# Score matmuls of 64 rows by 128 columns issued as 64 by 32 tiles

## Chip, cores and metric

The kernel runs on one core of a Trainium2 chip. The metric is the device time of one execution in microseconds (us), the median of several runs. A profile is taken of one further execution; its instruction trace is what the views below are read from.

## What is computed

One sequence of 2048 tokens with 512 channels goes through two attention blocks with 32 heads of 16 channels each. Block A is a linear attention with softmax features, block B is ordinary softmax attention. A gate per token mixes them. Cut to what matters:

```python
x = A_x                                              # [1, 2048, 512], bf16
g = sigmoid((x * gate_w).sum(-1, keepdims=True))
a = A(x)      # linear attention: phi(q) (phi(k)^T v) / (phi(q) . sum phi(k)), then @ A_wo
# B(x):
q, k, v = split_heads(x @ B_wqkv)                    # 32 heads, 16 channels
scores = einsum("bhqd,bhkd->bhqk", q, k) * 16 ** -0.5
p = softmax(scores, axis=-1)
b = einsum("bhqk,bhkd->bhqd", p, v) @ B_wo
out = g * a + (1 - g) * b
```

The 32 x 2048 x 2048 exponentials of block B are most of the work.

## The kernel before

**Work of block B.** The queries are cut into four chunks of 512. The heads stand in four groups of eight (`g`), and each group is gone through in two halves (`par`), so there are 32 "sets" of four heads and 512 queries (`N_SETS`). In each set the 16 tiles of 128 keys (`kt`) are gone through in two halves (`cc`), which makes 32 x 16 x 2 = 1024 score groups.

A score group (`qk`, L1103 to L1109, matmul on L1106) makes the scores of two heads: for each head 128 keys by 512 queries, into one PSUM bank per head. Keys of eight heads lie on the 128 partitions of `kT`. The queries lie in `qz`, spread out so that a slot holds one head of each half of the partitions and zeros elsewhere. One matmul uses the 64 partitions 0 to 63 (head half h = 0), the other 64 to 127 (h = 1). `tile_position=(64 * h, 0)` places each on its own half of the rows of the TensorE array, with all 128 columns of the array as output rows.

The exponential of the scores is made in one of two ways. For most key tiles ScalarE makes it (L1116), one instruction for the two banks of a group, from PSUM to the bf16 buffer `E`. For up to six of the 16 key tiles of a set VectorE makes it by arithmetic on the bit pattern: two instructions (L1121) per group, one for each bank, into the int16 buffer `T`, and two shifted copies `TS` (L1129), so that three terms stand for one exponential.

The value matmuls (`pv`, L1143) follow: four matmuls side by side, each with all 128 rows and a strip of 32 columns of the array (`tile_position=(0, 32 * col)`), which accumulate into the bank `psO`. A column of ones beside the values gives the sum for the softmax. A group of these is due once for each key tile that ScalarE made and three times for each one that VectorE made. At a set's end `psO` is copied out (L770), transposed by a DMA and normalised (L1169, L1170).

**PSUM.** Seven banks (`psR`) are shared by score groups, projections and all else; the eighth is `psO`. A score group for ScalarE takes two neighbouring banks, one for VectorE any two.

**The rest.** Projections of q, k, v (L787 and L849), the features of block A (L979 on ScalarE, L985 to L995 on POOL), its output (L1055), the output projection (L1205), a sum for a check of the value range (L927), and the gate (L892, one output column per matmul) are set in between as full 128 x 128 matmuls.

**What sets the order.** A planner in the program (`_Sched`) places every operation on an engine before the program is built, from a list of costs and due times written in the code: a score group counts 0.22 us, an exponential of ScalarE 0.905, a change of tiling on TensorE 0.11 (`SWITCH`). It writes one fixed list per engine; each engine runs its list in that order and waits on semaphores for what an operation needs. An operation made of several matmuls waits ahead of the first and signals with the last. The costs in the planner are not changed, so neither are the lists.

Of the kernel before, what the change touches and what calls it, by code (L numbers as in the profile page):

```python
# [101 lines left out]
class _Sched:  # L102
# [5 lines left out]
    def add(self, eng, prio, occ, fn, deps=(), tiles=(), mode=None, name="", lat=None, dma=None, lane=None, nb=0.0,  # L108
            kind=None, run=None, alt=None):
        o = _Op()  # L110
        o.alt = alt
        o.eng, o.fn, o.occ, o.prio = eng, fn, occ, prio
        o.lat = {"pe": 0.17, "act": 0.12, "dve": 0.09, "pool": 0.1, "sp": 0.0}[eng] if lat is None else lat
        if dma is not None:
            o.lat = dma
        o.deps = [d for d in deps if d is not None]
        o.tiles = list(tiles)
        o.mode, o.name, o.dma, o.lane, o.est, o.kind, o.run = mode, name, dma, lane, nb, kind, run
        o.users, o.start, o.end, o.count, o.sem, o.vc = [], None, None, None, None, None
        o.seq = len(self.ops)  # L120
        for t in o.tiles:
            t.ops.append(o)
        self.ops.append(o)
        return o
# [502 lines left out]
def _build(ctx, nc, A_x, A_wqkv, A_w_phi, A_wo, B_wqkv, B_wo, gate_w, out):  # L627
    cnt = [0]

    def sb(shape, dt=BF16, name="sb"):  # L630
        cnt[0] += 1
        return ctx.enter_context(nc.sbuf_tensor(f"{name}_{cnt[0]}", shape, dt))
# [13 lines left out]
    kT = sb([128, KT, S], name="kT")  # L646
# [52 lines left out]
    def pair(ts):  # L699
        return banks[:, ts[0].idx:ts[0].idx + 2, :]  # L700

    def st_(x):
        return T0 + P_SET * x
# [297 lines left out]
    for qd in range(4):  # L1001
# [13 lines left out]
        for lo in (0, 4):  # L1015
# [4 lines left out]
                start=(i == 0), stop=(i == 3)) for g in range(lo, lo + 4) for i, it in enumerate(items)]  # L1020
# [58 lines left out]
    for s in range(N_SETS):  # L1079
        qc, g, par = s // 8, (s // 2) % 4, s % 2  # L1080
# [5 lines left out]
        qt = q_t[g, qc]  # L1086
# [5 lines left out]
        for eng, frac, kt in todo:  # L1092
            alt = ((s, kt), eng) if kt in dset else None
            pr = st_(s + frac)
            T, T1, T2 = (_Tile(T_r), _Tile(TS_r), _Tile(TS_r)) if eng == "dve" else (None, None, None)
            exps, es = [], []
            for cc in range(2):
                rs = [_Tile(B_r), _Tile(B_r)]
                if eng == "act":
                    rs[0].mate, rs[1].mate = rs[1], rs[0]  # L1100
                c = 2 * par + cc

                def qk(e, rs=rs, c=c, kt=kt, g=g, qt=qt):  # L1103
                    ins = None
                    for h in range(2):
                        ins = e.matmul(rs[h].ap, lhsT=kT[64 * h:64 * h + 64, g, 128 * kt:128 * (kt + 1)],  # L1106
                                       rhs=qt.ap[64 * h:64 * h + 64, c, :], start=True, stop=True, tile_position=(64 * h, 0))
                    return ins
                q = add("pe", pr + 0.5 * cc, 0.22, qk, deps=[ev_k[g, kt // 4]] + (op_qz[g, qc] if len(op_qz[g, qc]) == 8 else [op_qz[g, qc][c]]), tiles=rs + [qt], mode="row",  # L1109
                        name=f"qk{s}.{kt}", kind="qk", run=eng, alt=alt)  # L1110
                if s == N_SETS - 1 and eng == "act":
                    tail_qk.append(q)
                if eng == "act":
                    E = _Tile(E_r)
                    es.append(E)
                    exps.append(add("act", pr + 0.5 * cc, 0.905, lambda e, rs=rs, E=E: e.activation(  # L1116
                        E.ap.rearrange("p (a n) -> p a n", n=512), pair(rs), ACTF.Exp, scale=SCALE),
                                    deps=[q], tiles=rs + [E], name="exp", kind="exp", alt=alt))
                else:
                    for h in range(2):  # L1120
                        exps.append(add("dve", pr + 0.5 * cc + 0.01 * h, 0.6, lambda e, rs=rs, T=T, cc=cc, h=h: e.tensor_scalar(  # L1121
                            T.ap[:, 1024 * cc + 512 * h:1024 * cc + 512 * h + 512], rs[h].ap,
                            ACC, BIAS, op0=ALU.mult, op1=ALU.add),
                            deps=[q], tiles=[rs[h], T], name="expd", kind="exp" if h else "exp0", alt=alt))
            if eng == "act":
                rounds = [(exps, lambda cc, es=es: es[cc].ap, lambda hd, kt=kt: vB[:, kt, hd, :], [], es)]
            else:
                di = DSET.index(kt)
                s1, s2 = (add("dve", pr + 1.0 + 0.3 * m, 0.6, lambda e, T=T, X=X, m=m: e.tensor_single_scalar(  # L1129
                    X.ap, T.ap, SHIFT[m], ALU.add), deps=exps, tiles=[T, X], name="sh", kind="sh", alt=alt) for m, X in ((1, T1), (2, T2)))  # L1130
                rounds = [(exps, lambda cc, T=T: T.ap[:, 1024 * cc:1024 * (cc + 1)].bitcast(BF16), lambda hd, kt=kt: vB[:, kt, hd, :], [], [T]),
                          ([s1], lambda cc, T=T1: T.ap[:, 1024 * cc:1024 * (cc + 1)].bitcast(BF16),
                           lambda hd, di=di: vS[:, 0, di, hd, :], [op_vS[g, kt // 4, 0]], [T1]),
                          ([s2], lambda cc, T=T2: T.ap[:, 1024 * cc:1024 * (cc + 1)].bitcast(BF16),
                           lambda hd, di=di: vS[:, 1, di, hd, :], [op_vS[g, kt // 4, 1]], [T2])]
            for ri, (dps, rhs, lhs, more, holds) in enumerate(rounds):
                def pv(e, rhs=rhs, lhs=lhs, g=g, par=par, O=O, s=s, key=(kt, ri)):
                    ins = None
                    for cc in range(2):
                        for h in range(2):  # L1140
                            col = 2 * h + cc
                            hd = 8 * g + 4 * h + 2 * par + cc
                            ins = e.matmul(O.ap[32 * col:32 * col + VW, :], lhsT=lhs(hd), rhs=rhs(cc)[:, 512 * h:512 * (h + 1)],  # L1143
                                           start=(first_pv[s] == key), stop=(last_pv[s] == key), tile_position=(0, 32 * col),
                                           skip_group_check=True)
                    return ins
                o = add("pe", pr + 2.5 - 40.0 * (s == N_SETS - 1), 0.22, pv, deps=list(dps) + [ev_v[g, kt // 4], op_psO] + more, tiles=holds + [O], mode="col",
                        name=f"pv{s}.{kt}.{ri}", kind="pv", alt=alt)
                o.run = (s, (kt, ri))
                pvs.append(o)  # L1150
# [153 lines left out]
```

## Time and profile before

| | |
|---|---|
| median of 3 runs | 748.07 us (747.75 to 748.65) |
| the profiled execution | 749.46 us, span of its instructions 747.6 us |
| mean granted TensorE clock | 0.992 of full speed |
| L1106 score matmuls | 2048, mean 386 ns, together 347.5 us of TensorE time |
| L1106 weight loads for them | 2048, mean 93 ns |
| L1143 value matmuls | 1452 + 1192 + 596, mean 382 to 384 ns |
| L1116 exponentials on ScalarE | 726, mean 1120 ns |
| L1121 first terms on VectorE | 596, mean 683 ns |

How to read it: PE is TensorE, PEld its weight loads, DVE is VectorE, ACT is ScalarE, POOL is GpSimd. Tile names read out<-in: `psR<-qz,kT` are the score matmuls, `psO<-E,vB` value matmuls. Matmuls are pipelined and the end of each is modelled, so the 386 ns of one matmul are its passage through the array, and several overlap; what one adds is read from the distance of the starts. The chain is the work that ended last, followed back from the last instruction: each step goes to what released it or to the instruction before it on its engine.

### The profile page before, as it was taken

To read this page: it belongs to the slowest core of one execution; us is meant where nothing else is said; L and a number is where in the kernel's file an instruction comes from. 1 tells how busy PE (TensorE), PEld (TensorE's weight loads), DVE (VectorE), ACT (ScalarE), POOL (GpSimd) and SP (SyncE) were. 2 spreads that over 40 slices of the span, in tenths; PEclk is the share of its full clock that TensorE was granted. 3 is DMA by queue.
4 is the path that set the end of the run, shared out by engine and by line. 5 is a ranking of instruction groups with operands and counts; after the bars stand their busy time and mean duration, and the time that the engine had idled before them with its cause. 6 is when DMAs were issued, how large, how long until landed. Compare 5 with 4: busy or idle time off the path is not lost.

```text
span 747.6 us, 15606 instructions
## 1 busy us (share of the span) xinstructions
PE 695.1 (93%) x6432; PEld 216.0 (29%) x6432; DVE 693.4 (93%) x1212; ACT 711.6 (95%) x803; POOL 193.7 (26%) x234
## 2 busy tenths in 40 slices
PE   7999999999999989988989999998989999988886
PEld 3333342332322222222222332222222322222222
DVE  3989899999999999999999999999999999999993
ACT  3999799999999999999999999999999999999993
POOL 4165241233344343322322012222212112200000
PEclk8999999999999999999999999999999999999999
DMA  8300000011000000001211221211111211111001
GB/s 210 73 16 9 8 16 15 15 41 33 15 15 15 8 14 10 15 16 30 48 31 30 50 50 36 44 33 33 22 36 40 47 36 37 32 27 8 16 8 32
DMA packets 72157, 23.77 MB, mean 32 GB/s; under 512 B 64016, under 2 KB 72080, under 8 KB 72080
## 3 DMA queue, kind: packets, MB, share of 16 engines
q1 hardware_dynamic: 70736, 22.19, 13.9%
q8 instruction: 52, 0.85, 0.5%
q10 hardware_dynamic: 1344, 0.52, 0.3%
q14 instruction: 25, 0.20, 0.1%
HBM read 4.21 MB, written 2.10 MB: 8 GB/s over the span
## 4 chain that ended last, share of the span: by engine, by line
ACT 65%; PE 26%; DVE 5%; DMA 2%; SPq 1%; issue 0%; DVEq 0%
ACT E L1116 62%; PE psR L1106 10%; PE psO L1143 6%; PE psR L787 4%; PE psR L1205 3%; DVE T L1121 2%; PE psR L849 2%; ACT WAT L979 2%; ACT phk L979 1%; DMA OTT<-OT 1%; DVE TS L1129 1%; SPq L706 1%; DMA T<-in_A_x_dram 1%; PE psR L927 1%; DVE ob L1170 1%
## 5 line engine op out<-in xcount | busy, mean ns | idle before, releaser
L1116 ACT ACTIVATE E<-psR 128x1024 bf16<-128x1024 f32 x726 | 679.8, 1120 | 17.2 <-PE psR L1106 15.8
L1121 DVE TENSOR_SCALAR T<-psR 128x512 int16<-128x512 f32 x596 | 380.8, 683 | 20.8 <-PE psR L1106 16.3
L1106 PE MATMUL psR<-qz,kT 64*128 64x512 bf16 x2048 | 347.5, 386 | 38.3 <-ACT E L1116 28.0
L1129 DVE TENSOR_SCALAR TS<-T 128x2048 int16<-128x2048 int16 x298 | 193.2, 684 | 3.1
L1106 PEld LDWEIGHTS psR<-qz,kT 64*128 64x128 bf16 x2048 | 87.0, 93 | 306.6 <-ACT E L1116 221.3
L1143 PE MATMUL psO<-E,vB 128*18 128x512 bf16 x1452 | 127.1, 382 | 0.0
L1143 PE MATMUL psO<-TS,vS 128*18 128x512 bf16 x1192 | 105.6, 382 | 0.6 <-DVE TS L1129 0.6
L1143 PE MATMUL psO<-T,vB 128*18 128x512 bf16 x596 | 58.7, 384 | 0.0
L985 POOL TENSOR_TENSOR WAT<-WAT 128x512 f32<-128x512 bf16 x16 | 18.5, 1156 | 148.0 <-DVE TS L1129 105.6
L990 POOL TENSOR_TENSOR tr<-WAT 128x256 f32<-128x256 f32 x32 | 23.4, 733 | 94.5 <-DVE TS L1129 94.5
L1143 PEld LDWEIGHTS psO<-E,vB 128*18 128x18 bf16 x1452 | 31.3, 88 | 51.3 <-issue 37.1
L995 POOL TENSOR_TENSOR phk<-phk,ss 128x1024 bf16<-128x1024 bf16 x16 | 30.9, 1930 | 51.5 <-DVE TS L1129 51.5
L995 POOL TENSOR_TENSOR WAT<-WAT,ss 128x1024 bf16<-128x1024 bf16 x16 | 30.9, 1930 | 48.5 <-DVE TS L1129 48.5
L1143 PEld LDWEIGHTS psO<-TS,vS 128*18 128x18 bf16 x1192 | 26.6, 87 | 53.3 <-issue 29.5
L787 PE MATMUL psR<-Wp,xT 128*128 128x512 bf16 x128 | 33.2, 382 | 0.8 <-DVE T L1121 0.8
L787 PE MATMUL psR<-xT,WB 128*128 128x512 bf16 x128 | 33.2, 382 | 0.4 <-ACT WAT L979 0.2
L985 POOL TENSOR_TENSOR WAT<-phk 128x512 f32<-128x512 bf16 x16 | 18.7, 1166 | 31.2 <-DVE TS L1129 31.2
L1143 PEld LDWEIGHTS psO<-T,vB 128*18 128x18 bf16 x596 | 14.5, 87 | 27.9 <-issue 21.4
L862 POOL TENSOR_SCALAR vS<-vB 128x144 bf16<-128x144 bf16 (+1 forms) x32 | 11.9, 373 | 39.4 <-DVE TS L1129 34.0
L770 DVE CAST OT<-psO 128x512 bf16<-128x512 f32 x31 | 21.1, 681 | 0.1
L979 ACT ACTIVATE phk<-psR 128x512 bf16<-128x512 f32 x32 | 18.6, 675 | 0.8 <-PE psR L787 0.8
L979 ACT ACTIVATE WAT<-psR 128x512 bf16<-128x512 f32 x32 | 19.1, 709 | 0.0
(108 smaller groups left out, 379.7 us busy)
## 6 DMA issues: line engine op xcount, KB each, us to landing
qz<-qst SPq DMA_DIRECT2D x120, 16.0 KB, 1.8
out_dram<-WAv SPq DMA_DIRECT2D x12, 128.0 KB, 1.7
WB<-in_B_wqkv_dram SPq DMA_DIRECT2D x3, 384.0 KB, 6.7
T<-in_A_x_dram SPq DMA_DIRECT2D x2, 512.0 KB, 5.3
WAv<-in_A_wqkv_dram SPq DMA_DIRECT2D x1, 512.0 KB, 8.3
WB<-in_A_wo_dram SPq DMA_DIRECT2D x1, 512.0 KB, 3.9
WB<-in_B_wo_dram SPq DMA_DIRECT2D x1, 512.0 KB, 3.6
OTT<-OT SPq DMA_TRANSPOSE x31, 2.4
```

The lines of the kernel that those rows point to most:

```text
L770: return add("dve", prio, 0.6, lambda e: e.tensor_copy(dst(), src()), deps=deps, tiles=tiles, name=name)
L787: calls = [lambda e, t=t: e.matmul(tile.ap[:, off:off + 512], lhsT=lhs(t), rhs=rhs(t), start=(t == 0), stop=(t == KT - 1)) for t in range(KT)]
L979: ex = [add("act", prio, 0.48, lambda e, s=s: e.activation(ev()[:, :, 16 * s:16 * s + 16], P(), ACTF.Exp, scale=1.0 - 2.0 * s), deps=[f] + ...
L985: p1 = pool(prio + 2, 1.23, lambda e: e.tensor_tensor(v8(), eg()[:, :, 0:8], eg()[:, :, 8:16], ALU.add), ex + use_wat, tiles=[ee, tr], nam ...
L990: p2 = pool(prio + 2, 0.92, lambda e: e.tensor_tensor(u4(), v8()[:, :, 0:4], v8()[:, :, 4:8], ALU.add), [p1], tiles=[tr, tr2])
L995: return pool(prio + 6, 1.95, lambda e: e.tensor_tensor(eg(), eg(), ss.ap[:, 1, :].unsqueeze(2).to_broadcast([128, 64, DH]), ALU.mult), [o ...
L1106: ins = e.matmul(rs[h].ap, lhsT=kT[64 * h:64 * h + 64, g, 128 * kt:128 * (kt + 1)], rhs=qt.ap[64 * h:64 * h + 64, c, :], start=True, stop= ...
L1116: exps.append(add("act", pr + 0.5 * cc, 0.905, lambda e, rs=rs, E=E: e.activation(E.ap.rearrange("p (a n) -> p a n", n=512), pair(rs), ACT ...
L1121: exps.append(add("dve", pr + 0.5 * cc + 0.01 * h, 0.6, lambda e, rs=rs, T=T, cc=cc, h=h: e.tensor_scalar(T.ap[:, 1024 * cc + 512 * h:1024 ...
L1129: s1, s2 = (add("dve", pr + 1.0 + 0.3 * m, 0.6, lambda e, T=T, X=X, m=m: e.tensor_single_scalar(X.ap, T.ap, SHIFT[m], ALU.add), deps=exps, ...
L1143: ins = e.matmul(O.ap[32 * col:32 * col + VW, :], lhsT=lhs(hd), rhs=rhs(cc)[:, 512 * h:512 * (h + 1)], start=(first_pv[s] == key), stop=(l ...
L1205: calls = [lambda e, tile=tile, off=off, sl=sl, src=src, w=w, n=n: e.matmul(tile.ap[:, off:off + 512], lhsT=src.ap[:, n % 4, sl], rhs=w[:, ...
```

## The change

Each of the two matmuls of a score group is cut into four along the 128 keys, which are the columns of the array. Each of the four has its own weight load of 32 columns and runs on a tile of 64 rows by 32 columns at `(64 * h, 32 * j)`. It streams the same 64 partitions by 512 queries and writes 32 partitions of the same PSUM bank as before. The two heads alternate.

```diff
                 def qk(e, rs=rs, c=c, kt=kt, g=g, qt=qt):
                     ins = None
-                    for h in range(2):
-                        ins = e.matmul(rs[h].ap, lhsT=kT[64 * h:64 * h + 64, g, 128 * kt:128 * (kt + 1)],
-                                       rhs=qt.ap[64 * h:64 * h + 64, c, :], start=True, stop=True, tile_position=(64 * h, 0))
+                    for j in range(4):
+                        for h in range(2):
+                            ins = e.matmul(rs[h].ap[32 * j:32 * j + 32, :], lhsT=kT[64 * h:64 * h + 64, g, 128 * kt + 32 * j:128 * kt + 32 * j + 32],
+                                           rhs=qt.ap[64 * h:64 * h + 64, c, :], start=True, stop=True, tile_position=(64 * h, 32 * j))
                     return ins
```

## The prediction

> **What bounds the kernel now.** I read the page's engine sums and its chain first, then the groups, the waits, and last the TensorE timeline around 302 us.
>
> ```profile
> span 747.6 us, 15606 instructions
> PE 695.1 (93%) x6432; PEld 216.0 (29%) x6432; DVE 693.4 (93%) x1212; ACT 711.6 (95%) x803; POOL 193.7 (26%) x234
> ...
> ACT 65%; PE 26%; DVE 5%; DMA 2%; SPq 1%; issue 0%; DVEq 0%
> ACT E L1116 62%; PE psR L1106 10%; PE psO L1143 6%; PE psR L787 4%; PE psR L1205 3%; DVE T L1121 2%; PE psR L849 2%; ACT WAT L979 2%; ACT phk L979 1%; DMA OTT<-OT 1%; DVE TS L1129 1%; SPq L706 1%; DMA T<-in_A_x_dram 1%; PE psR L927 1%; DVE ob L1170 1%
> ...
> L1116 ACT ACTIVATE E<-psR 128x1024 bf16<-128x1024 f32 x726 | 679.8, 1120 | 17.2 <-PE psR L1106 15.8
> L1106 PE MATMUL psR<-qz,kT 64*128 64x512 bf16 x2048 | 347.5, 386 | 38.3 <-ACT E L1116 28.0
> ```
>
> ScalarE is busy for 711.6 of 747.6 us and holds 65% of the chain that ended last: the exponentials of L1116 bound the kernel. TensorE holds 26% of that chain, so in about a quarter of the span its own order of work is late and ScalarE waits for it or is about to. The score matmuls (L1106), the only ones that change, are 10% of the chain, about 75 us.
>
> From the list of waits:
>
> ```profile
> PEld psR L1106 <- ACT E L1116: 221.3, 520, 0.8
> ...
> PEld psR L1106 <- DVE T L1121: 30.0, 94, 1.8
> ```
>
> Each row is total us, times, longest. There are 2048/2 = 1024 score groups of two matmuls. Some 520 + 94 = 614 of them begin when ScalarE or VectorE gives a PSUM bank back, not when TensorE gets to them. Up to such a wait, lateness gathered on TensorE is forgiven.
>
> The timeline of TensorE shows what a group costs (start, length of the merged piece, count):
>
> ```profile
> 302.31 0.39 PE L1106 MATMUL psR<-qz,kT 64*128 64x512 bf16 x2
> 302.63 0.39 PE L1143 MATMUL psO<-TS,vS 128*18 128x512 bf16 x4
> 302.85 0.39 PE L1143 MATMUL psO<-E,vB 128*18 128x512 bf16 x4
> 303.17 0.61 PE L1106 MATMUL psR<-qz,kT 64*128 64x512 bf16 x4
> 304.14 0.39 PE L1106 MATMUL psR<-qz,kT 64*128 64x512 bf16 x2 [0.37 <-ACT E L1116]
> 304.47 1.04 PE L787 MATMUL psR<-Wp,xT 128*128 128x512 bf16 x4
> 305.44 0.39 PE L1106 MATMUL psR<-qz,kT 64*128 64x512 bf16 x2
> ```
>
> Two things are to be seen. A second score group adds 0.61 - 0.39 = 0.22 us, and a second value group (L1143) starts 302.85 - 302.63 = 0.22 after the first, though one holds two matmuls and the other four: the tiles of a group run side by side. A step between tilings takes longer: 302.63 - 302.31 and 303.17 - 302.85 are 0.32, 304.47 - 304.14 is 0.33. So a change of tiling costs about 0.10 us, and it costs that also from 64x128 to 128x128 tiles (304.14 to 304.47), where the rows of a tile alone change.
>
> **The change part by part.**
>
> *Count.* Each of the 1024 score groups goes from 2 matmuls and 2 weight loads to 8 and 8: 6144 more of each, 12,576 of each on TensorE in all. The written order of all five engines is unchanged (one list per engine; only the members of a score group multiply), and so are the waits: the first matmul of a group waits, the last one signals. No DMA of the program, no tile and no buffer changes. VectorE, ScalarE and POOL do the same instructions.
>
> *Streaming.* If all eight 64x32 tiles run side by side the group still streams 512 columns, the 0.22 of above. The trace has no 64x32 tile. It has two row tiles beside each other (L1106) and four column tiles beside each other (L1143: four matmuls in one 0.39 piece). I cost the stream at nothing. If it does not hold, that is the second rival below.
>
> *Start of the later tiles.* Counting TensorE's instructions in 10 ns windows around the value group that starts at 301.71 gives x2, x4, x6 (two of each belong to the score group before), so its four matmuls start inside 20 ns: some 3 to 4 ns apart. In a score group the second starts within 10 ns. Eight tiles at 3 to 4 ns put the last one 21 to 28 ns behind the first, where it is 4 ns now: **+20 ns** on the group's end. From below this is 0, if starts got closer; from above the nearest row is L892, 32 pairs of load and one-column matmul in 0.95 us, less the 0.16 that one of them takes to pass: 0.79/31 = 25 ns a pair, which would make 7 x 25 - 4 = +171 ns. I take 20, since L1143 is the column-tiled stream and L892 reuses one tile, so each must follow the one before.
> The Trainium skill (TensorE: Matmul & The Clock Gate, Measured speedup vs the span model) gives about 4 ns per added tile; by it the six added tiles cost 24 ns, and the sum below would be 6.0 us in place of 5.0.
>
> *Weight loads.* Steps into a value group (four loads of 18 columns) and into a score group (two of 128) both take 0.32, so neither count nor width of loads shows. Eight of 32 columns I cost at 0, bounded by the 10 ns that two such steps differ by.
>
> *Switches.* A score group is still tiled otherwise than the value matmuls (64 against 128 rows) and than the projections. Rows alone differing cost 0.33 above, so no switch goes: 0.
>
> *Instruction supply.* The two instruction queues carried 1.05 MB for 15,606 instructions in the whole span, at 0.6% of the DMA engines. 12,288 more add about 0.8 MB. TensorE must then be handed 25,152 in 747.6 us, one every 30 ns, where it is 58 now. Cover: the densest piece seen, L892, takes one every 12.5 ns. If that pace is not sustained, the first rival follows.
>
> *What reaches the end.* 75 us of score matmuls on the chain at 0.22 (no switch) to 0.32 (switch) a group are 235 to 340 groups; most stand at a switch, so about 250. Each ends 20 ns later: 250 x 0.020 = **5.0 us**, and this is a floor if 20 ns holds, since the order is fixed and the chain is only lengthened. The ceiling is all groups, 1024 x 0.020 = 20.5. Groups off the chain are mostly those 614 that start at a released bank; there the 20 ns is hidden by ScalarE's next exponential (L1116, 1120 ns), whose input lies ready. Some groups between them will join the chain, as from 37 to 75 us, where 25 of 52 groups wait for a bank (from 300 to 338 us it is 47 of 55). I add 1.5 us for these, near the floor because more than half of the groups wait. Sum +6.5: the profiled execution took 749.46 around its span of 747.6, and goes to 756.0; against the median 748.07 of the runs shown this is 754.5.
>
> **The rivals.**
>
> 1. *TensorE is not handed instructions fast enough.* For: 16 per group in place of 4, and rows show no stretch longer than 64 instructions at the dense pace. Against: steps of 3 ns in value groups, and no wait on TensorE in the page that nothing explains. Price at L892's 25 ns a pair: +171 ns on 250 groups, 43 us, so 791; on all 1024, 175 us, so 923. The same page of the Trainium skill (Wait — 56ns, not 53.3ns?) states about 62 ns per matmul where instructions are decoded by the sequencer's code. An estimate by that page is 8 x 62 = 496 ns a group, and the time would pass 900; no run here shows which decoding is in use.
>
> 2. *The two row halves do not run together once columns are split.* Then a group takes two passes, +0.21 us: 250 x 0.21 = 53, so 801; on all, 218, so 966. For: no row has both kinds at once. Against: each kind alone runs at full overlap.
>
> 3. *Nothing reaches the end.* The 20 ns ends in the 614 waits each time, or starts get closer together: below 1.5 us, 748. Against: the chain has about 250 such groups in stretches where TensorE does not wait.
>
> 4. *Faster: the switch between score and value groups goes*, since both are now four column tiles. Place: L1106 to L1143 and back. Price: 0.10 us each, up to 25 us off the 250 groups on the chain. ScalarE's floor limits it: even if all 15.8 us of waits of L1116 for scores went, 747.6 - 15.8 = 732 remains, and 5.4 of them are at the start, so about 737. It decides as soon as a step from score to value group falls under 0.30. For: the column split becomes equal. Against: rows alone differing (L1106 to L787) cost as much today.
>
> **How the numbers follow.** Chances: forecast 0.66 (own range 751 to 770, floor 5.0 with a little less to the ceiling 20.5), rival 1 0.12, rival 2 0.05, rival 3 0.11, rival 4 0.06. Predicted is the forecast's 754.5. The range takes the forecast, rival 3 and the lower end of rival 1: 747 to 791. Left out are rival 4, rival 2 and half of rival 1, 0.17. A measurement of this kernel tells about 0.2% (1.5 us) from no change: faster 0.06, same 0.11, slower 0.83.
>
> **What would show it.** Right: a score row of 8192 matmuls with a mean near 380 ns; a lone group's piece of about 0.41 in place of 0.39, a second group still adding 0.22; the step from score to value group 0.34 in place of 0.32; more and longer waits of L1116 for scores than 28 and 15.8 us; ScalarE's busy time unchanged. A piece of 0.55 for a lone group means rival 1, 0.60 with starts in two packs rival 2, a step of 0.24 between score and value group rival 4, the same waits as before rival 3. What would make me wrong: a start distance of eight mixed tiles unlike that of four, loads that no longer hide, or stretches of TensorE that become the chain as a whole.

## The result and the profile after

The changed kernel takes 752.68 us (median of 6 runs, 751.28 to 753.76) against 748.36 us for the kernel before, measured beside it: ratio 1.0052, 95% interval 1.0031 to 1.0072. Repeated later beside other kernels it was 1.0054 (1.0039 to 1.0070). The two ratios stand for 3.9 and 4.0 us; 4.0 is used below. 6.5 was predicted and 5.0 named as a floor.

The same parts of the page, of the kernel after:

```profile
span 749.9 us, 27894 instructions
PE 704.4 (94%) x12576; PEld 232.2 (31%) x12576; DVE 695.1 (93%) x1212; ACT 713.4 (95%) x803; POOL 193.3 (26%) x234
...
ACT 65%; PE 28%; DVE 4%; DMA 1%; SPq 1%; issue 0%; POOL 0%
...
L1117 ACT ACTIVATE E<-psR 128x1024 bf16<-128x1024 f32 x726 | 681.4, 1095 | 17.1 <-PE psR L1107 15.6
L1107 PE MATMUL psR<-qz,kT 64*32 64x512 bf16 x8192 | 359.8, 386 | 31.9 <-ACT E L1117 22.0
```

8192 score matmuls of 386 ns each, as before, and TensorE's idle time in front of them down from 38.3 to 31.9 us: TensorE has used up some of its waits. The share of TensorE in the chain went from 26 to 28%. From the list of waits:

```profile
PEld psR L1107 <- ACT E L1117: 203.9, 485, 0.8
...
PEld psR L1107 <- DVE T L1122: 31.9, 99, 1.8
...
ACT E L1117 <- PE psR L1107: 15.6, 30, 4.7
```

584 groups wait for a bank, where 614 did. The last row had this form before:

```profile
ACT E L1116 <- PE psR L1106: 15.8, 28, 5.4
```

Here two of the signs named for a right forecast did not come: the waits of the exponentials for scores were to become more and longer, and are 30 with 15.6 us where 28 had 15.8; and ScalarE's busy time was to stay, and went from 711.6 to 713.4 us. By the sign "the same waits as before" alone one would have called rival 3. This list does not show the loss. It stands in the distances between exponentials all the same: 687 of them follow directly on another one, and the distances of their starts add up to 650.6 us in place of 648.1, where the spans of the two profiled executions differ by 2.3.

TensorE's timeline of the same piece of work:

```profile
303.14 0.41 PE L1107 MATMUL psR<-qz,kT 64*32 64x512 bf16 x8
303.48 0.39 PE L1144 MATMUL psO<-TS,vS 128*18 128x512 bf16 x4
303.70 0.39 PE L1144 MATMUL psO<-E,vB 128*18 128x512 bf16 x4
304.02 0.63 PE L1107 MATMUL psR<-qz,kT 64*32 64x512 bf16 x16
304.97 0.41 PE L1107 MATMUL psR<-qz,kT 64*32 64x512 bf16 x8 [0.33 <-ACT E L1117]
```

A lone group is 0.41 long in place of 0.39, a second one adds 0.63 - 0.41 = 0.22 as before, the step from a score to a value group is 303.48 - 303.14 = 0.34 in place of 0.32, and the one back is still 0.32 (304.02 - 303.70). The eight starts lie 3.3 ns apart, 23 ns from first to last; before it was 3 to 4.

One thing had no line in the prediction. Where ScalarE stands idle for a score group, the time from the group's first matmul to the exponential can be read directly. Before, then after, at the same instruction (the 406th exponential):

```profile
427.56 0.61 PE L1106 MATMUL psR<-qz,kT 64*128 64x512 bf16 x4
428.00 1.02 ACT L1116 ACTIVATE E<-psR 128x1024 bf16<-128x1024 f32 x1 [0.26 <-PE psR L1106]
```

```profile
428.67 0.63 PE L1107 MATMUL psR<-qz,kT 64*32 64x512 bf16 x16
429.15 1.02 ACT L1117 ACTIVATE E<-psR 128x1024 bf16<-128x1024 f32 x1 [0.34 <-PE psR L1107]
```

The exponential starts 0.44 us after the group's first matmul before (0.431 at full resolution, and the same in nearly all such places), and 0.48 after (0.482). That is 50 ns, not the 20 of the later starts. The semaphore's own records say why: the update comes 14 ns after the modelled end of the last matmul where one full tile runs, 19 ns with two row tiles (score groups before), 30 ns with four column tiles (value groups) and 49 ns with eight (score groups after), about 5 ns for each tile. Counted from a group's first start, the median update comes at 409 ns before and at 459 ns after.
The Trainium skill (TensorE: Matmul & The Clock Gate, The cost: per-tile semaphore tail) gives 4.7 ns a tile and 26.3 ns for each matmul of the pack that raises a semaphore. An estimate by it is 28 ns for six tiles more; the trace has 30 (19 to 49).

### The profile page after: what moved, and what is told of

It reads as the page before. It is cut to its first block, busy times and chain, and to the rows that moved or that the text cites. A ratio compares the mean times of both kernels' runs of the same rounds, so it can differ in the third digit from the quotient of the medians.

```text
span 749.9 us, 27894 instructions
## 1 busy us (share of the span) xinstructions
PE 704.4 (94%) x12576; PEld 232.2 (31%) x12576; DVE 695.1 (93%) x1212; ACT 713.4 (95%) x803; POOL 193.3 (26%) x234
## 4 chain that ended last, share of the span: by engine, by line
ACT 65%; PE 28%; DVE 4%; DMA 1%; SPq 1%; issue 0%; POOL 0%
ACT E L1117 62%; PE psR L1107 11%; PE psO L1144 7%; PE psR L787 4%; PE psR L1206 3%; PE psR L849 2%; ACT WAT L979 2%; DVE T L1122 2%; ACT phk L979 1%; SPq L706 1%; DMA T<-in_A_x_dram 1%; DVE TS L1130 1%; PE psR L927 1%; DMA Wp<-WAT 1%; DVE ob L1171 1%
## 5 line engine op out<-in xcount | busy, mean ns | idle before, releaser
L1117 ACT ACTIVATE E<-psR 128x1024 bf16<-128x1024 f32 x726 | 681.4, 1095 | 17.1 <-PE psR L1107 15.6
L1122 DVE TENSOR_SCALAR T<-psR 128x512 int16<-128x512 f32 x596 | 382.2, 684 | 22.4 <-PE psR L1107 18.3
L1107 PE MATMUL psR<-qz,kT 64*32 64x512 bf16 x8192 | 359.8, 386 | 31.9 <-ACT E L1117 22.0
L1107 PEld LDWEIGHTS psR<-qz,kT 64*32 64x32 bf16 x8192 | 102.2, 89 | 293.4 <-ACT E L1117 203.9
```

Of the source, the lines that this page charges most:

```text
L1107: ins = e.matmul(rs[h].ap[32 * j:32 * j + 32, :], lhsT=kT[64 * h:64 * h + 64, g, 128 * kt + 32 * j:128 * kt + 32 * j + 32], rhs=qt.ap[64 * ...
```

## The experiments

Two theories at first: the later starts lengthen TensorE's own steps out of a score group, and that reaches the end (the prediction's); or the cost goes with the number of instructions, with cut columns as such, or with the later signal to ScalarE and VectorE. On TensorE's list 491 of the 1024 score groups are followed by a score group and 533 by something of another tiling.

**Cutting only some of the groups (sw_only and qk_only).** `before_qk` holds the groups that are followed by a score group; one kernel cuts the others, one cuts these.

```diff
+                    n = 4 if (me in before_qk) == False else 1     # == True in the second kernel
+                    w = 128 // n
-                    for j in range(4):
+                    for j in range(n):
...
-                            ins = e.matmul(rs[h].ap[32 * j:32 * j + 32, :], ..., tile_position=(64 * h, 32 * j))
+                            ins = e.matmul(rs[h].ap[w * j:w * j + w, :], ..., tile_position=(64 * h, w * j))
```

> Only the 533 score groups that are followed on TensorE by something other than a score group are cut into 64x32 tiles; the other 491 keep their two 64x128 matmuls. Theory (the last tile of a group starts 20 ns later, and what follows with another tiling waits for it, so TensorE's own order carries the delay): nearly the whole effect, 1.004 to 1.0055 against the kernel before. Rival one (the cost goes with the number of instructions or weight loads): 533/1024 of it, about 1.0027. Rival two (the consumers' later signal carries it, whatever follows on TensorE): about half, 1.002 to 1.003.

Measured 1.0156 (1.0143 to 1.0170), three times the whole change.

> The other half: only the 491 score groups that are followed by a score group are cut. Theory: the next group's first tile starts as early as before (0.226 us after the first start of this one), so TensorE's order loses nothing and only the signal to ScalarE or VectorE is 20 ns later: 1.000 to 1.001. Rivals one and two: 491/1024 of the effect, 1.002 to 1.003.

Measured 1.0129 (1.0112 to 1.0145). Both expectations failed, and with them the design: neighbouring score groups now have different tilings and pay a switch that no kernel had before. Of the 491 steps from a score to a score group 387 and 385 took 0.30 us or more, 178 before; the median is 0.320 and 0.342, where 0.226 is the step without a wait. So 64x32 beside 64x128 costs the same 0.1 us as a change of rows, and these two runs can't tell the theories apart.

**Half the cut (cols64).** Four tiles of 64 by 64.

```diff
-                    for j in range(4):
+                    for j in range(2):
...
-                            ins = e.matmul(rs[h].ap[32 * j:32 * j + 32, :], ..., tile_position=(64 * h, 32 * j))
+                            ins = e.matmul(rs[h].ap[64 * j:64 * j + 64, :], ..., tile_position=(64 * h, 64 * j))
```

> Every score group as four 64x64 tiles. Theory: starts 3.3 ns apart put the last one 10 ns behind the first in place of 4, a third of the added 20: 1.0015 to 1.002, and the step from a score to a value group about 0.327 us against 0.32 and 0.34. Rival (columns that are cut at all put TensorE into a dearer tiling, whatever the number): the whole 1.005.

Measured 1.0059 (1.0046 to 1.0072): as much as eight tiles, and so a miss for the theory at first sight. TensorE's timeline of this kernel:

```profile
302.83 0.41 PE L1107 MATMUL psR<-qz,kT 64*64 64x512 bf16 x4
303.17 0.39 PE L1144 MATMUL psO<-TS,vS 128*18 128x512 bf16 x4
303.39 0.39 PE L1144 MATMUL psO<-E,vB 128*18 128x512 bf16 x4
303.71 0.63 PE L1107 MATMUL psR<-qz,kT 64*64 64x512 bf16 x8
```

The starts are 10 ns apart in all, but the piece is 0.41 and the step to a value group 0.34 here (it is 0.316 in three cases of ten and 0.340 in the others), and a score group behind a score group comes after 0.240 in place of 0.226. So a group behind a group loses 14 ns here, where eight tiles of 32 columns lose none (0.226 in the changed kernel too). Loads of 64 columns that don't hide fit this; that was not tried by itself. The signal comes 26 ns later in the mean.

**Tiles of fewer rows (rows32).** The columns stay 128, each matmul takes only the 32 rows that hold its head, and the heads are dealt to the two halves of a set so that the two groups of a key tile use different rows.

```diff
-                c = 2 * par + cc
+                c = 2 * cc + par
...
-                        ins = e.matmul(rs[h].ap, lhsT=kT[64 * h:64 * h + 64, ...], rhs=qt.ap[64 * h:64 * h + 64, c, :], ..., tile_position=(64 * h, 0))
+                        r = 64 * h + 32 * (c // 2)
+                        ins = e.matmul(rs[h].ap, lhsT=kT[r:r + 32, ...], rhs=qt.ap[r:r + 32, c, :], ..., tile_position=(r, 0))
...
-                            hd = 8 * g + 4 * h + 2 * par + cc
+                            hd = 8 * g + 4 * h + 2 * cc + par
...
```

> The other way to make tiles smaller: 128 columns stay, and each score matmul takes only the 32 rows that hold its head, the two heads of a set's first half in other rows than those of its second half, so that four tiles of two score groups have rows of their own. Theory: a score group that follows one with other rows need not wait for the array, its step falls from 0.226 us to about 0.01 wherever no bank is missing, and the chain loses some of its 0.22 steps: 0.985 to 0.997, not under 737 us, where ScalarE alone bounds. Rival: rows of another group wait all the same, step 0.226 and 1.000.

Measured 1.0167 (1.0136 to 1.0198). The step fell where it could, but not everywhere: in the order of TensorE's list 309 of the 491 score groups behind a score group use other rows than the one before, and 182 use the same. Of the 309, 85 start about 7 ns after the group before, 60 after 20 to 200 ns only 14 after 200 to 250, and the others later, as waits; of the 182, 86 still take 200 to 250 ns. And the clock did not stay. Stretches of 10 us of this kernel (busy time of each engine with counts, then the granted clock of TensorE, the DMA share and GB/s):

```profile
330.00:340.00 10.00, 8.65 (x91) 2.30 (x86) 9.78 (x18) 10.00 (x13) 3.35 (x4) 1.00 0.13 26
340.00:350.00 10.00, 9.43 (x82) 2.66 (x74) 8.45 (x17) 9.21 (x12) 1.16 (x1) 0.83 0.15 29
350.00:360.00 10.00, 9.47 (x66) 1.60 (x66) 6.90 (x13) 7.60 (x8) 3.35 (x4) 0.51 0.15 31
```

At half clock ScalarE, the engine that bounds, falls to 7.60 of 10 us. The mean clock is 0.966 in the profiled execution, 0.944 to 0.966 in the runs, and 0.991 to 0.997 for the kernel before. Whether fewer rows at work or less streaming takes the clock away is open. So is what this kernel would do at full clock; an estimate from its own six runs, which differ by 0.32 us for each 0.001 of mean clock, is that the clock accounts for about 11 of its 12 us.

**Lengthening the groups without a new tiling (tail_sw and tail_qk).** The kernel before, whose score groups write their first 128 queries a second time, at the 533 switches (tail_sw) or at the 491 others (tail_qk). This adds work and leaves the values as they are.

```diff
                     for h in range(2):
                         ins = e.matmul(rs[h].ap, ..., tile_position=(64 * h, 0))
+                    for h in range(2 if (me in before_qk) == False else 0):      # == True in the second kernel
+                        ins = e.matmul(rs[h].ap[:, 0:128], ..., rhs=qt.ap[64 * h:64 * h + 64, c, 0:128], ..., tile_position=(64 * h, 0))
```

> The changed kernel once more, beside the next three on one chip: 1.004 to 1.007.

Measured 1.0054 (1.0039 to 1.0070).

> The kernel before, with 64x128 tiles, but the 533 score groups that are followed on TensorE by another tiling repeat their first 128 queries (the same values written again), which makes the group about 56 ns longer. Theory (only the lengthening of TensorE's own steps counts, 36 to 43% of it reaching the end as in the changed kernel, where 533 x 20 ns = 10.7 us gave 3.9 to 4.5): 30 us of steps, 10 to 14 us, 1.014 to 1.018. Rival (the later signal to ScalarE and VectorE counts, whatever follows on TensorE): 533/1024 of 2.8 times the effect, 5.5 to 6.5 us, 1.008.

Measured 1.0094 (1.0081 to 1.0107), 7.0 us. The steps out of these 533 groups grew by 56 ns as meant (median to a value group 0.319 to 0.375).

> The same lengthening at the 491 score groups that are followed by a score group. About half of these steps wait for a bank anyway, so about 245 steps grow by 56 ns, 14 us. Theory: 4.5 to 6 us, 1.006 to 1.009, under half of the one at the switches. Rival (signals): nearly as much as at the switches, ratio 491 to 533.

Measured 1.0045 (1.0032 to 1.0058), 3.4 us; steps from 0.226 to 0.282. The ratio of the two, 2.1, is near the one that the steps give (533 against some 270 that don't wait), not the 1.09 of the signals. But both sizes are well below what the theory expected from the changed kernel: 23% of the added step time reaches the end here, and it was taken to be 40%. So the changed kernel must have a cost besides its steps.

**As many instructions, other tiles (nsplit).** Eight matmuls a group, on the two 64x128 tiles, four of 128 queries after one another.

```diff
-                    for h in range(2):
-                        ins = e.matmul(rs[h].ap, ..., rhs=qt.ap[64 * h:64 * h + 64, c, :], ...)
+                    for j in range(4):
+                        for h in range(2):
+                            ins = e.matmul(rs[h].ap[:, 128 * j:128 * j + 128], ..., rhs=qt.ap[64 * h:64 * h + 64, c, 128 * j:128 * j + 128], ...)
```

> As many matmuls and weight loads as in the changed kernel (8 each per score group), but on the two 64x128 tiles: four matmuls of 128 queries one after the other in place of one of 512. Theory: only steps count; four times 53 + 2.5 ns in place of 216 makes them 8 ns longer, 533 + 245 steps give 6 us, of which 2 to 3 reach the end: 1.002 to 1.004. Rival (the number of instructions): at least the 1.005 of the changed kernel, with steps that grow by more than 8 ns or waits that nothing else explains.

Measured 1.0023 (1.0012 to 1.0034), with steps 8 ns longer and the signal 6 ns later. It has the 27,894 instructions of the changed kernel and half of its cost, so their number makes at most that half, and the steps and the signal account for most of this half too (see the table below).

**The signal alone (inc2 and inc8).** In the kernel before, the first matmul of a group raises a semaphore that nobody reads; in a second kernel (inc8) seven of the eight matmuls of a changed group do.

```diff
                     for h in range(2):
                         ins = e.matmul(rs[h].ap, ..., tile_position=(64 * h, 0))
+                        if h == 0:
+                            ins.then_inc(spare, 1)
```

> The kernel before, but the first matmul of every score group also raises a semaphore that nobody reads. Nothing of the steps on TensorE should change; the group's own signal should come some 26 ns later. Theory two (the changed kernel loses by two things: its steps out of score groups, 20 ns each, and its signal, which comes 49 ns after the one of before; worked out from the changed kernel and the tail at switches at 0.19 of the summed steps and 0.048 of the summed signal delay): 1024 x 26 ns = 27 us, of which 1.3 us reach the end, 1.001 to 1.0025. Theory one (TensorE's steps alone): 1.000.

Measured 1.0033 (1.0020 to 1.0047), 2.5 us, with score-to-value steps no longer than before (median 0.319) and the signal 26 ns later (median 434 ns after the first start in place of 409). The exponential of above, in this kernel:

```profile
427.05 0.61 PE L1106 MATMUL psR<-qz,kT 64*128 64x512 bf16 x4
427.51 1.02 ACT L1118 ACTIVATE E<-psR 128x1024 bf16<-128x1024 f32 x1 [0.29 <-PE psR L1106]
```

0.46 in place of 0.44, and ScalarE idle for 0.29 in place of 0.26. TensorE does nothing else than before; only the signal is late. By itself this speaks against the theory of the steps alone; some of the 2.5 us goes with the clock (see below), the rest does not.

> The changed kernel, but all eight matmuls of a group raise a semaphore, seven of them one that nobody reads: signal some 180 ns later than in the changed kernel, steps unchanged. Theory two: at least 0.048 x 1024 x 180 ns = 9 us on top of the changed kernel, 1.017 or more. Theory one: 1.005, as the changed kernel.

Measured 1.0390 (1.0372 to 1.0408): 25 us on top of the changed kernel, for a signal that comes 195 ns later still (mean 653 ns), with the usual steps of the changed kernel (0.34 to a value group, 0.226 to a score group). This refutes the theory of the steps alone. The page of this kernel shows TensorE and VectorE taking over the chain:

```profile
PE 40%; ACT 37%; DVE 17%; DMA 2%; SPq 2%; issue 1%; POOL 0%
ACT E L1119 35%; PE psR L1107 20%; DVE T L1124 11%; PE psO L1146 10%; PE psR L787 5%; DVE TS L1132 4%; PE psR L1208 2%; PE psR L849 1%; SPq L706 1%; DMA T<-in_A_x_dram 1%; ACT phk L979 1%; ACT WAT L979 1%; SPq L835 1%; DVE ob L1173 1%; DMA Wp<-WAT 1%
```

**Steps and signal at about the size of the change (tail48).** The kernel before with 48 queries of every group written twice.

```diff
+                    for h in range(2):
+                        ins = e.matmul(rs[h].ap[:, 0:48], ..., rhs=qt.ap[64 * h:64 * h + 64, c, 0:48], ..., tile_position=(64 * h, 0))
```

> The kernel before, with the first 48 queries of every score group written a second time: steps and signal of all groups about 20 ns later. Theory two: steps 20 ns x (533 + 270) = 16 us x 0.19 = 3.0 us and signal 20.5 us x 0.048 = 1.0 us, together 1.005. Theory one: 16 us at the 0.4 of the changed kernel, 6.5 us, 1.0085.

Measured 1.0070 (1.0052 to 1.0088), between the two; theory two's number is just outside the interval and theory one's inside. As measured it does not decide.

**The two terms together.** Steps are the change of the usual step out of a group times the groups that don't wait there (and, in the two column-tiled kernels, 2 to 3 ns less for each step into one); signal is the change of its mean delay times 1024. "Two terms" is 0.18 x steps + 0.055 x signal, close to the best fit to these seven (0.18 and 0.06, standard errors 0.03 and 0.016). The last column is explained behind the table:

| kernel | steps, us | signal, us | measured, us | two terms, us | measured, at equal clock, us |
|---|---|---|---|---|---|
| change | 9.1 | 50.2 | 4.0 | 4.4 | 3.7 (the repeat) |
| cols64 | 10.9 | 27.0 | 4.4 | 3.4 | 3.4 |
| tail_sw | 29.8 | 28.2 | 7.0 | 6.9 | 7.5 |
| tail_qk | 15 | 24.8 | 3.4 | 4.1 | 4.4 |
| nsplit | 6.2 | 6.3 | 1.7 | 1.5 | 1.6 |
| tail48 | 18.3 | 20.9 | 5.2 | 4.4 | 4.1 |
| inc2 | 0 | 26.5 | 2.5 | 1.5 | 1.5 |

No row is off by more than 1.1 us; single results are uncertain by 0.8 to 1.3. By these terms the change's 4.0 us are about 1.6 of steps and 2.8 of signal, together 4.4. The division is only as good as the fit. It holds for delays of this size: for inc8 the same terms would give 11 us over the changed kernel, where 25 were measured.

Much of what the rows are off by goes with the clock. Each run has its own mean granted clock on record, and among the runs of one kernel the time follows it: over the 101 runs of the kernels other than rows32 for which both are known, 0.41 us for each 0.001 of clock (standard error 0.02, correlation -0.88). The kernels compared did not have the same clock: 0.994 for the kernel before in the batch of inc2, inc8 and tail48 and 0.992 for these three, 0.995 for tail_qk and 0.992 for the kernel before beside it. The last column is an estimate that takes this out at that rate, to about 0.2 us (one standard error). Two readings change. inc2 costs 1.5 us, not 2.5, and still more than nothing; and tail48 costs 4.1 us, 1.0055, which is near theory two's 1.005 and away from theory one's 1.0085. Fitted to this column the terms are 0.20 and 0.04 (standard errors 0.013 and 0.007), and no row is off by more than 0.5 us. Whether a kernel's tiles move its clock by these few thousandths, or chance does, is not shown.

## Why the prediction was right, and where it was not

- *Count and order*: as predicted, 12,576 matmuls and loads, order unchanged.
- *Streaming*: as predicted; eight tiles of 64x32 stream together, a second group adds 0.22. Rival 2 is out (its price for all groups, 218 us, is 215 by its own 0.21).
- *Start of the later tiles*: 23 ns from first to last in place of 3 to 4, so +20 ns as taken.
- *Weight loads*: costed at 0. The usual step into a score group even fell, from 0.322 to 0.319 after a value group and from 0.312 to 0.309 after a projection. That loads never show is refuted as a rule only if the 14 ns of cols64 are theirs.
- *Switches*: as predicted, 0.34 out of a score group and 0.32 into one; rival 4 is out. That rows alone cost a switch was read rightly; the mixed kernels showed that columns alone do too.
- *Instruction supply*: starts 3.3 ns apart and nsplit put rival 1 out.
- *What reaches the end*: here two sizes were wrong, in opposite directions, and that the time came out near the forecast is in part luck. The group's end was put 20 ns later for everyone. For TensorE's next step to another tiling that holds, but for ScalarE and VectorE the signal is 49 ns later, since it also trails the last matmul by 5 ns for each tile that ran beside it. The row stood in the trace of before (14, 19 and 30 ns for one, two and four tiles); only the starts were read.
- Against this, "250 x 0.020 = 5.0 us, a floor" was no floor. Followed back link by link, the chain of before does hold 250 score groups. But "most stand at a switch" misread it: only 120 of them are followed on the chain by another tiling, 110 by a score group, and 20 hand over to ScalarE or VectorE. A score group behind a score group starts 0.226 us after it before and after the change, as the prediction itself had it ("a second group still adding 0.22"). So the 20 ns fall on 120 links, 2.4 us, and the 49 ns of the signal on 20, 1.0 us: an estimate of 3.4 us, where 4.0 were measured.
- Not every link of a chain is a step that must be, either. The chain counts a matmul group as following the one before when their modelled 0.39 us overlap, although only 0.22 to 0.32 of it is the step. A group that waited for a bank by less than the 0.07 to 0.17 us that are left then looks like a link of TensorE's own. In the trace of before 111 of the 120 steps to another tiling have the length without a wait, and 71 of the 110 to a score group. Together these 182 would make 10.2 us of the 56 ns of tail_sw and tail_qk, which cost 10.4 together; all 250 would have made 14.
- Rival 3 (nothing reaches the end) is out by the time alone: even the lower end of the interval, 2.3 us, is above its 1.5.
- The added 1.5 us for groups that join the chain has no counterpart that could be measured by itself. The errors cancel in part: 6.5 predicted, 4.0 measured.

## What to carry to other kernels

Cutting a matmul into narrower tiles that stream together left its 0.22 us of streaming alone here, but each of the six tiles more put the group's signal about 8 ns later (3.3 of start, 5 of tail; two more tiles of 64x64 put it 13 ns later each), so cut only where a tile brings in work that would else be streamed after. Price a delay twice: by what it adds to the engine's own next step, and by what it adds to the signal that another engine waits for. On a chain, ask of each link what follows it: a delay of a group's end counts only where the next step waits for that end. Where differences are below one per cent, compare the granted clocks of the runs too. Before one part of a tiling change is undone, look whether neighbours of unlike tiling then pay a switch that neither kernel had.

## What the runs showed of the hardware that was not expected

- An update that nobody waits for is not free on TensorE: one more matmul of a group that raises a semaphore put the group's real signal 26 ns later, seven put it 195 ns later, 28 ns each. The delays had been expected at about this size; that seven cost 25 us, over twice what the small delays would give, had not.
- A change of columns alone (64x128 beside 64x32) takes the same 0.1 us as a change of rows.
- Score groups on rows of their own can start 7 ns after one another, though they belong to different operations; in that kernel the granted clock fell to 0.51 in a stretch of 10 us with TensorE still 0.95 busy in the profile.
- Among runs of one kernel the time followed the granted clock, 0.41 us for each 0.001: the scatter of 0.93 us about each kernel's mean falls to 0.45 when this is taken out.
